# The loads of the first six tiles in the order of the program text

## The chip, the cores and the metric

The kernel runs on one core of a Trainium2 chip. A time is the device time in microseconds from the first to the last instruction of one execution. Where several runs are given, the median is taken.

## The reference

Four batches, eight heads, 768 positions, head size 64. Each head attends to 8 global positions and to the last 96 positions, with a linear penalty on the distance. The heads' results, joined to 512 features, go through a feed-forward block with a time shift.

```python
scores = scale * np.matmul(q, k.transpose(0, 1, 3, 2)) - slopes * dist
scores = np.where(keep, scores, -1000000000.0)
a = softmax(scores)
x = np.matmul(a, v)                      # heads joined: [4, 768, 512]
xk = mu_k * x + (1.0 - mu_k) * x_prev    # x_prev: x one position earlier
xr = mu_r * x + (1.0 - mu_r) * x_prev
k = np.maximum(xk @ w_k, 0.0)
out = sigmoid(xr @ w_r) * (k * k @ w_v)
```

`w_k` is 512 x 1024, `w_v` 1024 x 512, `w_r` 512 x 512. They arrive as 64-bit words, two 32-bit integers for each value.

## The kernel before

**Tiles.** The 4 x 768 positions are 24 tiles of 128. A tile is loaded (`load_tile`: q and k; `load_v`: v, as `va` and `vb`), then goes through `scores` in four pairs of heads (L424 to L428 on TensorE, bias and row maximum on VectorE at L433, exponential on ScalarE at L434, scaling by the reciprocal `r` on GpSimd at L450 or ScalarE at L448), `transposes` (L462, copied by ScalarE at L464) and `weighted`, the products with v (L481, copied to `x` at L492). Tiles 0 to 5 use q and k as they are loaded (64 partitions, names `qz` and `kz`); later ones are split in a high and a low part first (`qraw`, `kraw`, L297 on GpSimd, L403 and L404 on VectorE).

**Feed-forward.** Two tiles make a chunk. `mix` forms xk and xr with a high and a low part (L505 to L510); the low part of the first chunk's xk is `xk_lo`, on VectorE at L510. `channel_mix` multiplies with the weights in three products each (L517, L518, L519): `kp` for w_k, `z` for w_r, `vps` for w_v. The second product of each `kp` step (L518) reads `xk_lo`.

**Weights.** Ten blocks of 1 MB, w_0 to w_3 of `w_k`, w_4 and w_5 of `w_r`, w_6 to w_9 of `w_v`. `weight_load` brings one in (L181, L182). `weight_begin` makes a 32-bit float of the two integers in three steps on VectorE (L210, L211, L212) and casts it to the high part on ScalarE (L216). `weight_end` makes the low part: over TensorE (L230, L231), or by a subtraction at L234, on VectorE, and for w_4 and w_5 on GpSimd. The table `PLAN` says which.

**Order.** The program text is a loop over steps; each step loads the next tile, runs the score stage of one tile, the value products of an earlier one, some of the feed-forward, and one or two weight blocks. A scheduler takes the instructions in this order, estimates when each could start, and places them anew on each engine's queue. What an engine executes is then that fixed order. All loads go through SyncE's one queue, where an instruction that has to wait holds those behind it. A load waits for the readers of its buffer (q has two buffers, `qz_0` and `qz_1`, k three, v two), and for the landing of an earlier load whose semaphore it takes over; there are eight of these.

Of the kernel before, what the change touches and what calls it, by code (L numbers as in the profile page):

```python
# [62 lines left out]
def tile_biased_attention_channel_mix(ctx: ExitStack, tc: tile.TileContext, qT, kT, v, n_sizes, mu_kr, w_k, w_v, w_r, q_rows, k_rows, v_rows, slopes, out):  # L63
# [215 lines left out]
    def weights_load(n):  # L279
        while w_count[2] < min(n, len(w_steps)):  # L280
            weight_load(w_count[2])
            w_count[2] += 1

    def weights_go(begun, ended):
        weights_load(begun)
        while w_count[0] < min(begun, len(w_steps)):
            weight_begin(w_count[0])
            w_count[0] += 1
        while w_count[1] < min(ended, w_count[0]):
            weight_end(w_count[1])  # L290
            w_count[1] += 1
# [41 lines left out]
    def first_keys(n):  # L333
        if n % NT:
            (vec.tensor_copy if n in PLAN.get("KC", ()) else pool_copy)(state[n - 1]["kr"][0:64, :, 128 - OWN : 128 - BACK], k_first)
        else:
            pool_copy(k_first, state[n]["kr"][0:64, :, 0:GMAX])

    def load_tile(n):
        b, t = divmod(n, NT)  # L340
        s = state[n] = {}
        native = n < NATIVE
        halves = (0,) if native else (0, 64)
        if native:
            qr, kr = q_zero[n % 2], k_ring[n % 3]
        else:
            qr = p4k.tile([128, H, 128], F32, tag="t4k", name=f"qraw_{n}")
            if n == NATIVE:
                kr = kw_pool.tile([128, H, W], F32, tag="kw", name=f"kraw_{n}")
            else:  # L350
                kr = p4k.tile([128, H, 128], F32, tag="t4k", name=f"kraw_{n}")
        for o in halves:
            q_load[n] = nc.sync.dma_start(qr[o : o + 64], qT[n])
        for o in halves:
            if n == NATIVE:
                nc.sync.dma_start(kr[o : o + 64, :, OWN:W], kT[n])
                if t:
                    nc.sync.dma_start(kr[o : o + 64, :, 0:GMAX], kT[n - t, :, :, 0:GMAX])
                    nc.sync.dma_start(kr[o : o + 64, :, GMAX:OWN], kT[n - 1, :, :, 32:128])
            else:  # L360
                nc.sync.dma_start(kr[o : o + 64], kT[n])
        s["qr"], s["kr"] = qr, kr

    def load_v(n):

        g = PLAN.get("VB", {}).get(n)
        if g in q_load:
            with tc.issue_after(q_load[g].ins):
                load_v_now(n)
        else:  # L370
            load_v_now(n)
# [14 lines left out]
    def split_tile(n):  # L386
        t = n % NT
        s = state[n]
        s["sum"] = s_pool.tile([128, H], F32, name=f"sum_{n}", tag="sum")
        s["nmax"] = s_pool.tile([128, H], F32, name=f"nmax_{n}", tag="nmax")  # L390
        s["e"] = {}
        if n < NATIVE:
            return
        qh = q_pool.tile([128, H, 128], F32R, name=f"qh_{n}", tag="qh")
        ql = q_pool.tile([128, H, 128], F32R, name=f"ql_{n}", tag="ql")
        kw = kw_pool.tile([128, H, W], F32R, name=f"kw_{n}", tag="kw")
        cur = kw[:, :, 0 if n == NATIVE and t else OWN : W]
        kr = s["kr"]
        if n == NATIVE:
            kr = kr[:, :, W - cur.shape[2] : W]  # L400
        pool_copy(qh, s["qr"])
        pool_copy(cur, kr)
        vec.tensor_sub(ql, s["qr"], qh)  # L403
        vec.tensor_sub(cur[64:128], kr[64:128], cur[64:128])  # L404
        if t and n > NATIVE:
            pk = state[n - 1]["kw"]
            first = OWN if t == 1 else 0
            pool_copy(kw[:, :, GMAX:OWN], pk[:, :, OWN + 32 : W])
            pool_copy(kw[:, :, 0:GMAX], pk[:, :, first : first + GMAX])
        s["qh"], s["ql"], s["kw"] = qh, ql, kw  # L410
# [41 lines left out]
    def transposes(n, hp):  # L452
        s = state[n]
        parts = [128, W - 128] if n % NT else [128]
        nb = len(parts)
        pt = ps_t.tile([128, 512], F32, name=f"t_{n}_{hp}", tag="t")
        et = et_pool.tile([128, 512], F32, name=f"et_{n}_{hp}", tag="et")
        for u in range(2):
            e = s["e"].pop(2 * hp + u)
            for k, p in enumerate(parts):  # L460
                c = (2 * k + u) * 128
                pe.transpose(pt[0:p, c : c + 128], e[:, k * 128 : k * 128 + p], ident)  # L462
        for k, p in enumerate(parts):
            (vec.tensor_copy if (n, hp, k) in PLAN.get("ET", ()) else act.copy)(et[0:p, k * 256 : k * 256 + 256], pt[0:p, k * 256 : k * 256 + 256])  # L464
        s["et", hp] = et

    def weighted(n, hp):
        t = n % NT
        s = state[n]
        if hp == 0:  # L470
            s["av"] = ps_a.tile([128, 512], F32, name=f"av_{n}", tag="av")
        et = s.pop(("et", hp))
        blocks = s["va"]
        nb = len(blocks)
        for u in range(2):
            h = 2 * hp + u
            for k, vt in enumerate(blocks):

                q, c, p = k * LATE, (2 * k + u) * 128, vt.shape[0]
                o = s["av"][64 * u : 64 * u + 64, hp * 128 + q : (hp + 1) * 128]  # L480
                pe.matmul(o, vt[:, h * 64 : (h + 1) * 64], et[0:p, c + q : c + 128], start=k == 0, stop=k == nb - 1)  # L481
        if hp == 3:
            c, i = divmod(n, 2)
            if i == 0:
                xt = x_pool.tile([128, 4, 257], F32, name=f"x_{c}", tag="x")
                state["x", c] = xt
                if t == 0:
                    pool.memset(xt[:, :, 0:1], 0.0)
                else:
                    pool_copy(xt[:, :, 0:1], state["x", c - 1][:, :, 256:257])  # L490
            xt = state["x", c]
            (vec.tensor_copy if n in PLAN.get("XC", ()) else act.copy)(xt[:, :, 1 + 128 * i : 129 + 128 * i], s["av"].rearrange("p (a q) -> p a q", a=4))  # L492
# [81 lines left out]
    def ffn(c):  # L574
        xt = state["x", c]
        xk = mix(xt[:, :, 1:257], xt[:, :, 0:256], "k", p4k, f_pool, c < PLAN.get("MA", 1))
        xr = mix(xt[:, :, 1:257], xt[:, :, 0:256], "r", p4k, f_pool, c < PLAN.get("MA", 1))
        return channel_mix(xk, xr, lambda i: out[(2 * c + i) * 128 : (2 * c + i + 1) * 128, :], f_pool, f2_pool, ps_f, c >= 10, c == NCHUNK - 1)
# [7 lines left out]
    def run_ffn(amount):  # L586
        budget[0] += amount
        while budget[0] >= 1.0 and queue:
            try:
                next(queue[0])  # L590
                budget[0] -= 1.0
            except StopIteration:
                queue.pop(0)
        if not queue:
            budget[0] = 0.0

    load_tile(0)
    split_tile(0)
    for step in range(NTILES + 1):
        if step + 1 < NTILES:  # L600
            load_tile(step + 1)
        if step == 0:
            load_v(0)
        if step < NATIVE:
            first_keys(step)
        for hp in range(4):
            if hp == 0 and step > 1:
                for i in range(4):
                    weighted(step - 2, i)
            if hp == 0 and 0 < step < NTILES:  # L610
                load_v(step)
            if step:
                transposes(step - 1, hp)
            if step < NTILES:
                scores(step, hp)
            if hp == 0:
                if step >= LAG and (step - LAG) % 2 == 0:
                    queue.append(ffn((step - LAG) // 2))
                    if len(queue) == 1 and step == LAG:
                        budget[0] = PLAN.get("BUD", -17.5)  # L620
            run_ffn(2.5)
            run_ffn(2.5)
            if hp == 1 and step + 1 < NTILES:
                split_tile(step + 1)
            slot = 4 * step + hp
            weights_load(LOADS[min(slot, len(LOADS) - 1)])
            n = BEGUN[min(slot, len(BEGUN) - 1)]
            weights_go(n, n - 1 if slot < len(BEGUN) else n)
# [194 lines left out]
```

## Time and profile before

| | |
|---|---|
| median of 3 runs | 503.87 us (503.28 to 503.95) |
| the profiled execution, its span | 503.9 us |
| TensorE busy | 488.8 us, 97% |
| VectorE busy | 355.8 us, 71% |
| ScalarE busy | 344.6 us, 68% |
| GpSimd busy | 234.2 us, 46% |
| DMA moved | 60.57 MB, mean 120 GB/s |
| granted clock of TensorE | 0.998 |

The shares are means over the whole span. The first 50 us differ from the rest: there the weights and six tiles are loaded and the weights are prepared. In the rows, PE is TensorE, DVE VectorE, ACT ScalarE, POOL GpSimd and SP SyncE; an arrow [idle before <- releaser] gives the idle time just before an instruction and what ended it.

### The profile page before, as it was taken

What the parts mean: (1) busy time and instruction counts of PE and PEld (TensorE: products, weight loads), DVE (VectorE), ACT (ScalarE), POOL (GpSimd) and SP (SyncE); (2) the same over time, 40 slices, a digit from 0 to 9 for tenths busy, and PEclk for the clock granted to TensorE, in tenths of its full rate; (3) what the DMA queues carried; (4) which work ended last, traced back from release to release, by engine and by line L of the source; (5) the groups of instructions that cost most, each with busy time, mean ns of one, the idle gap of its engine ahead of it and who ended that gap; (6) DMA issues with size and microseconds to landing.
All of it is one profiled execution on the core that took longest, in us unless ns stands there. A gap on an engine that the chain in (4) does not pass through costs nothing.

```text
span 503.9 us, 10303 instructions
## 1 busy us (share of the span) xinstructions
PE 488.8 (97%) x3590; PEld 431.3 (86%) x3590; DVE 355.8 (71%) x843; ACT 344.6 (68%) x858; POOL 234.2 (46%) x371
## 2 busy tenths in 40 slices
PE   7978999999999999999999999999999999999996
PEld 4647988998998998998898998898898898897985
DVE  5999989868678668658678668658768755457441
ACT  7798888377587577567577677667577678587360
POOL 4537537645655635626546536527447435204000
PEclk9999999999999999999999999999999999999999
DMA  8999460714604604603603612613413215647311
GB/s 224 325 252 250 133 182 18 195 54 104 165 1 115 167 5 103 171 14 82 159 29 86 165 39 81 160 46 81 132 59 79 86 39 164 208 159 260 125 43 48
DMA packets 22586, 60.57 MB, mean 120 GB/s; under 512 B 3296, under 2 KB 4576, under 8 KB 22016
## 3 DMA queue, kind: packets, MB, share of 16 engines
q1 hardware_dynamic: 22384, 59.85, 41.5%
q8 instruction: 30, 0.49, 0.4%
q14 instruction: 28, 0.23, 0.2%
q10 hardware_dynamic: 144, 0.00, 0.0%
HBM read 53.55 MB, written 6.29 MB: 119 GB/s over the span
## 4 chain that ended last, share of the span: by engine, by line
PE 84%; DMA 7%; DVE 4%; POOL 3%; issue 1%; SPq 0%; POOLq 0%; DVEq 0%
PE kp L517 8%; PE vps L518 8%; PE vps L519 8%; PE kp L519 8%; PE vps L517 8%; PE kp L518 8%; PE av L481 7%; PE t L462 7%; PE z L517 4%; PE z L519 4%; PE z L518 4%; DMA qz<-in_qT_dram 4%; PE s L428 3%; PE s L427 3%; DMA qraw<-in_qT_dram 2%; POOL e L450 2%
## 5 line engine op out<-in xcount | busy, mean ns | idle before, releaser
L450 POOL TENSOR_SCALAR e<-e,r 128x232 f32<-128x232 f32 (+1 forms) x180 | 94.9, 545 | 152.5 <-DVE r L444 121.5
L517 PE MATMUL kp<-xk_hi,wk 128*128 128x256 f32 x384 | 108.4, 283 | 0.0
L518 PE MATMUL kp<-xk_lo,wk 128*128 128x256 f32 x384 | 107.3, 280 | 0.5 <-DVE xk_lo L510 0.5
L519 PE MATMUL kp<-xk_hi,wk 128*128 128x256 f32 x384 | 107.4, 280 | 0.0
L434 ACT ACTIVATE e<-e,nmax 128x232 f32<-128x232 f32 (+1 forms) x192 | 90.0, 472 | 24.6 <-DVE nmax L433 22.4
L433 DVE CUSTOM_DVE_ANT_0 e<-s,pat 128x232 f32<-128x232 f32 (+1 forms) x192 | 64.7, 374 | 18.6 <-PE s L428 15.7
L517 PE MATMUL vps<-wv,kk_hi 128*128 128x512 f32 (+1 forms) x200 | 76.7, 384 | 0.0
L519 PE MATMUL vps<-wv,kk_lo 128*128 128x512 f32 (+1 forms) x200 | 76.6, 383 | 0.0
L518 PE MATMUL vps<-wv,kk_hi 128*128 128x512 f32 (+1 forms) x200 | 76.4, 382 | 0.1
L518 PEld LDWEIGHTS kp<-xk_lo,wk 128*128 128x128 f32 x384 | 72.1, 188 | 1.3 <-DVE xk_lo L510 0.7
L517 PEld LDWEIGHTS kp<-xk_hi,wk 128*128 128x128 f32 x384 | 72.1, 188 | 0.8 <-issue 0.2
L519 PEld LDWEIGHTS kp<-xk_hi,wk 128*128 128x128 f32 x384 | 72.1, 188 | 0.0
L464 ACT COPY et<-t 128x256 f32<-128x256 f32 (+1 forms) x176 | 57.0, 373 | 8.1 <-PE t L462 7.5
L545 DVE TENSOR_TENSOR kk<-kp,kk 128x512 f32<-128x512 f32 x48 | 33.1, 689 | 40.8 <-ACT kk L544 40.5
L462 PE MATMUL t<-ident,e 128*128 128x128 f32 x352 | 55.9, 277 | 1.7 <-POOL e L450 1.6
L462 PEld LDWEIGHTS t<-ident,e 128*128 128x128 f32 x352 | 40.2, 135 | 12.3 <-POOL e L450 2.6
L547 DVE TENSOR_TENSOR kk_lo<-kk,kk_hi 128x512 fp32r<-128x512 f32 x48 | 34.0, 709 | 23.3 <-ACT kk_hi L546 23.0
L403 DVE TENSOR_TENSOR ql<-qraw,qh 128x1024 fp32r<-128x1024 f32 x18 | 35.1, 1951 | 13.7 <-POOL qh L297 13.7
L519 PEld LDWEIGHTS vps<-wv,kk_lo 128*128 128x128 f32 x200 | 37.6, 188 | 7.5
L518 PEld LDWEIGHTS vps<-wv,kk_hi 128*128 128x128 f32 x200 | 37.7, 189 | 6.6 <-DVE wv L234 0.2
L517 PEld LDWEIGHTS vps<-wv,kk_hi 128*128 128x128 f32 x200 | 37.7, 189 | 6.5 <-issue 0.2
L492 ACT COPY x<-av 128x512 f32<-128x512 f32 x24 | 14.2, 591 | 42.5 <-PE av L481 42.5
(115 smaller groups left out, 1105.6 us busy)
## 6 DMA issues: line engine op xcount, KB each, us to landing
qraw<-in_qT_dram SPq DMA_DIRECT2D x36, 256.0 KB
kraw<-in_kT_dram SPq DMA_DIRECT2D x36, 256.0 KB
out_dram<-sig SPq DMA_DIRECT2D x23, 256.0 KB
va<-in_v_dram SPq DMA_DIRECT2D x20, 240.0 KB
vb<-in_v_dram SPq DMA_DIRECT2D x20, 208.0 KB
w<-in_w_k_dram SPq DMA_DIRECT2D x4, 1024.0 KB
w<-in_w_v_dram SPq DMA_DIRECT2D x4, 1024.0 KB
again<-in_w_k_dram SPq DMA_DIRECT2D x8, 512.0 KB
```

Of the source, the lines that this page charges most:

```text
L403: vec.tensor_sub(ql, s["qr"], qh)
L433: biased[n, hp] = vec.tensor_tensor_reduce(out=e[:, :w], in0=o, in1=p[:, h, :], op0=ALU.add, op1=ALU.min, scale=-0.125, scalar=3.0e38, acc ...
L434: act.activation(e[:, :w], e[:, :w], AF.Exp, bias=s["nmax"][:, h : h + 1], scale=-1.0, accum_out=s["sum"][:, h : h + 1])
L450: pool.tensor_scalar(e[:, :w], e[:, :w], r[:, u : u + 1], 1.0, op0=ALU.mult, op1=ALU.mult)
L462: pe.transpose(pt[0:p, c : c + 128], e[:, k * 128 : k * 128 + p], ident)
L464: (vec.tensor_copy if (n, hp, k) in PLAN.get("ET", ()) else act.copy)(et[0:p, k * 256 : k * 256 + 256], pt[0:p, k * 256 : k * 256 + 256])
L481: pe.matmul(o, vt[:, h * 64 : (h + 1) * 64], et[0:p, c + q : c + 128], start=k == 0, stop=k == nb - 1)
L517: pe.matmul(o, sh, mh, start=first, stop=False)
L518: pe.matmul(o, sh, ml, start=False, stop=False)
L519: pe.matmul(o, sl, mh, start=False, stop=last)
L545: vec.tensor_mul(kk, pv, kk)
L547: rest = vec.tensor_sub(kkl[:, 2 * fp : 2 * fp + 2, :], kk, kkh[:, 2 * fp : 2 * fp + 2, :])
```

## The change

A mode of the scheduler that leaves an engine's instructions in the order of the program text is switched on for SyncE, before the first tile is loaded, and off again at step 6.

```diff
+    queue_order = ExitStack()
+    queue_order.enter_context(tc.manual_schedule(engines={mybir.EngineType.SP}))
     load_tile(0)
     split_tile(0)
     for step in range(NTILES + 1):
+        if step == 6:
+            queue_order.close()
         if step + 1 < NTILES:
             load_tile(step + 1)
```

On SyncE, from the blocks w_2 and w_3 (`w64_2`, `w64_3`) on; `qz_1` and `kz_0` are q and k of tile 3, `qz_0` and `kz_1` those of tile 4. Before:

```order
L181 DMA w64_2_300<-in_w_k_dram 128x2048
L181 DMA w64_3_357<-in_w_k_dram 128x2048
L383 DMA vb_2_405<-in_v_dram 104x512
L182 DMA w64_4_456<-in_w_r_dram 128x2x1024
L182 DMA w64_5_517<-in_w_r_dram 128x2x1024
L361 DMA kz_0_179<-in_kT_dram 64x1024
L353 DMA qz_1_182<-in_qT_dram 64x1024
L381 DMA va_2_404<-in_v_dram 8x512
L382 DMA va_2_404<-in_v_dram 120x512
L361 DMA kz_1_183<-in_kT_dram 64x1024
L353 DMA qz_0_178<-in_qT_dram 64x1024
```

The same stretch of the change:

```order
L181 DMA w64_2_302<-in_w_k_dram 128x2048
L181 DMA w64_3_359<-in_w_k_dram 128x2048
L353 DMA qz_1_182<-in_qT_dram 64x1024
L361 DMA kz_0_179<-in_kT_dram 64x1024
L381 DMA va_2_406<-in_v_dram 8x512
L382 DMA va_2_406<-in_v_dram 120x512
L383 DMA vb_2_407<-in_v_dram 104x512
L182 DMA w64_4_458<-in_w_r_dram 128x2x1024
L182 DMA w64_5_519<-in_w_r_dram 128x2x1024
L353 DMA qz_0_178<-in_qT_dram 64x1024
L361 DMA kz_1_183<-in_kT_dram 64x1024
L381 DMA va_3_549<-in_v_dram 8x512
```

q and k of tile 3, and `va_2`, moved from behind w_4 and w_5 to a place ahead of them. Further up in the queue, q of tile 2 now stands ahead of k of tile 2 and `va_1`.

On VectorE, the twelve rows that end with the first chunk's `xk_lo` (`wa_5` is block w_5 in preparation, `e_3_1` head 1 of tile 3). Before:

```order
L508 SCALAR_TENSOR_TENSOR mix_k_571<-x_0_401,mus_69,mix_k_571 128x256
L211 SCALAR_TENSOR_TENSOR wa_5_519<-w64_5_517,wa_5_519 128x1024
L433 ISA e_3_0_565,nmax_3_455<-s_3_0_560,pat_136 128x232
L433 ISA nmax_3_455 128x1
L433 ISA e_3_1_568,nmax_3_455<-s_3_0_560,pat_136 128x232
L433 ISA nmax_3_455 128x1
L212 SCALAR_TENSOR_TENSOR wa_5_519<-w64_5_517,wa_5_519 128x1024
L433 ISA e_3_2_610,nmax_3_455<-s_3_1_605,pat_136 128x232
L433 ISA nmax_3_455 128x1
L433 ISA e_3_3_613,nmax_3_455<-s_3_1_605,pat_136 128x232
L433 ISA nmax_3_455 128x1
L510 TENSOR_TENSOR xk_lo_573<-mix_k_571,xk_hi_572 128x1024
```

With the change, eleven rows from the first step of w_5 on:

```order
L210 TENSOR_SCALAR wa_5_521<-w64_5_519 128x1024
L433 ISA e_3_3_615,nmax_3_457<-s_3_1_607,pat_136 128x232
L433 ISA nmax_3_457 128x1
L212 SCALAR_TENSOR_TENSOR wa_4_460<-w64_4_458,wa_4_460 128x1024
L508 SCALAR_TENSOR_TENSOR mix_k_573<-x_0_403,mus_69,mix_k_573 128x256 x2
L433 ISA e_3_4_642,nmax_3_457<-s_3_2_637,pat_136 128x232
L433 ISA nmax_3_457 128x1
L433 ISA e_3_5_645,nmax_3_457<-s_3_2_637,pat_136 128x232
L433 ISA nmax_3_457 128x1
L211 SCALAR_TENSOR_TENSOR wa_5_521<-w64_5_519,wa_5_521 128x1024
L508 SCALAR_TENSOR_TENSOR mix_k_573<-x_0_403,mus_69,mix_k_573 128x256 x2
```

and, three rows further down, the twelve that end with `xk_lo`:

```order
L433 ISA nmax_3_457 128x1
L443 TENSOR_SCALAR r_3_1_618<-sum_3_456 128x4
L212 SCALAR_TENSOR_TENSOR wa_5_521<-w64_5_519,wa_5_521 128x1024
L210 TENSOR_SCALAR wa_6_648<-w64_6_627 128x1024
L433 ISA e_4_0_739,nmax_4_626<-s_4_0_734,pat_136 128x232
L433 ISA nmax_4_626 128x1
L433 ISA e_4_1_742,nmax_4_626<-s_4_0_734,pat_136 128x232
L433 ISA nmax_4_626 128x1
L444 RECIPROCAL r_3_1_618<-r_3_1_618 128x4
L210 TENSOR_SCALAR wa_7_781<-w64_7_696 128x1024
L211 SCALAR_TENSOR_TENSOR wa_6_648<-w64_6_627,wa_6_648 128x1024
L510 TENSOR_TENSOR xk_lo_575<-mix_k_573,xk_hi_574 128x1024
```

All of tile 3's bias steps, those of tile 4's first two heads, the first two steps of w_6 and the first of w_7 now stand ahead of `xk_lo`. On TensorE, the first three pairs of tile 4's scores, the last transposes of tile 2 and eleven of tile 2's sixteen value products moved ahead of the first L518. From tile 6 on the order is the same but for the buffer numbers.

## Rows read from the trace of the kernel before

**Rows 1.** Busy time by stretch, core 0: us, then busy (xinstructions) of each engine

```profile
20.00:46.20 26.20, 21.88 (x155) 16.32 (x153) 25.02 (x55) 23.13 (x64) 15.39 (x16) 1.00 1.00 290
46.20:95.00 48.80, 47.12 (x355) 41.35 (x356) 44.37 (x92) 38.07 (x93) 26.75 (x31) 1.00 0.48 130
95.00:400.00 305.00, 305.00 (x2292) 274.15 (x2290) 221.52 (x515) 208.82 (x517) 162.38 (x260) 1.00 0.34 93
400.00:503.90 103.90, 99.25 (x716) 88.81 (x712) 51.11 (x120) 60.12 (x139) 20.42 (x39) 0.99 0.39 130
sum 503.90, PE 488.82 PEld 431.28 DVE 355.76 ACT 344.56 POOL 234.25; mean PE 97.76 PEld 86.26 DVE 71.15 ACT 68.91 POOL 46.85
```

**Rows 2.** Waits of TensorE over the span: in total, times, longest

```profile
PE s L424 <- DMA qz<-in_qT_dram: 2.5, 1, 2.5
...
PE t L462 <- POOL e L450: 1.6, 2, 0.8
...
PE s L424 <- issue: 0.7, 1, 0.7
```

**Rows 3.** Timeline of SyncE's queue, 16 to 40 us: start, us, what

```profile
19.49 0.54 SPq L353 DMA_DIRECT2D qz<-in_qT_dram  x1
...
38.47 0.90 SPq L182 DMA_DIRECT2D w<-in_w_v_dram  x2
```

**Rows 4.** The chain that ended last, in order of time: start, us, piece

```profile
19.49 18.96 DMA qz<-in_qT_dram
...
39.72 0.20 PE s L424 x2
39.92 0.24 PE s L425 x2
...
41.07 0.45 PE t L462 x4
...
49.82 0.31 DVE e L433
...
51.59 0.61 DVE wa L210
...
52.27 0.39 DVE mix_r L508
52.66 1.14 DVE wa L212
...
93.82 1.80 PE av L481 x32
```

**Rows 5.** Timeline of VectorE to 95 us: start, us, instruction [idle before, releaser]

```profile
35.60 0.71 DVE L210 TENSOR_SCALAR wa<-w 128x1024 int32<-128x1024 int32 x1 [0.27 <-DMA w<-in_w_r_dram]
...
39.34 1.21 DVE L211 SCALAR_TENSOR_TENSOR wa<-w,wa 128x1024 int32<-128x1024 int32 x1
...
42.95 3.22 DVE L510 TENSOR_TENSOR xk_lo<-mix_k,xk_hi 128x1024 fp32r<-128x1024 f32 x1
46.10 3.08 DVE L210 TENSOR_SCALAR wa<-w 128x1024 int32<-128x1024 int32 x1
...
59.83 1.19 DVE L510 TENSOR_TENSOR xr_lo<-mix_r,xr_hi 128x1024 fp32r<-128x1024 f32 x1
```

**Rows 6.** Timeline of GpSimd to 95 us

```profile
39.21 3.50 POOL L450 TENSOR_SCALAR e<-e,r 128x232 f32<-128x232 f32 x3 [2.06 <-DVE r L444]
42.68 2.40 POOL L234 TENSOR_TENSOR wr<-wa,wr 128x1024 fp32r<-128x1024 f32 x1
...
46.23 2.40 POOL L234 TENSOR_TENSOR wr<-wa,wr 128x1024 fp32r<-128x1024 f32 x1
```

**Rows 7.** Busy time by stretch: the last two columns are DMA share and GB/s

```profile
30.00:36.00 6.00, 4.66 (x35) 2.57 (x30) 5.73 (x13) 5.97 (x19) 2.22 (x3) 1.00 1.01 198
...
48.00:50.00 2.00, 1.29 (x11) 0.85 (x11) 2.00 (x6) 0.90 (x4) 0.63 (x1) 1.00 0.61 127
```

**Rows 8.** Timeline of TensorE, 46 to 92 us

```profile
46.22 0.39 PE L518 MATMUL kp<-xk_lo,wk 128*128 128x256 f32 x1 [0.49 <-DVE xk_lo L510]
```

## The prediction

> **What bounds the kernel now.** I read busy time by stretch first, then the waits of TensorE, the chain of waits, and last the timelines of SyncE, VectorE and GpSimd from 16 to 64 us. The span is 503.9 us and TensorE is busy for 488.8 of it [rows 1]. By stretch its idle time lies at the two ends. From 95 to 400 us there is none (305.00 of 305.00), so whatever is late there is late behind TensorE [rows 1]. The last stretch holds 4.65 idle us (103.90 less 99.25), which belongs to the end of the kernel. The change can touch 20 to 46.2 us (26.20 less 21.88, 4.32 idle) and 46.2 to 95 us (48.80 less 47.12, 1.68 idle) [rows 1]. Six microseconds, 1.2% of the span, is therefore all that a better order of loads can win. A loss has no such bound.
>
> The longest wait in there is the one that the moved loads bear on: tile 3's scores wait 2.5 us for its q [rows 2]. The chain has that transfer as one piece of 18.96 us from 19.49, when SyncE issued it behind the two w_r blocks (w_4 and w_5) of 1 MB each [rows 3, 4]. The reader should see a second thing there. When q has landed, the chain doesn't stay on TensorE: it goes through the subtraction xk_lo on VectorE (42.95 to 46.2), and the first feed-forward products (kp) start 0.05 us behind it, at 46.22, after a wait for just that [rows 5, 8]. From there on TensorE has work enough. What ends the starved stretch is thus the time of the first xk_lo; an earlier q matters as far as it brings that forward.
>
> **The change part by part.** It adds and removes no work; it fixes the SyncE order of tiles 0 to 5, and the scheduler then places the other engines' instructions anew.
>
> SyncE. q and k of tile 3 move ahead of w_4 and w_5, as the order shows; so does va of tile 2. k of tile 2 and va of tile 1 move back behind q of tile 2, which waits for tile 0's scores. I cost that last move at nothing: w_0 and w_1 (2.1 MB) are still under way then and cover it. The same transfers as before stand ahead of w_2 and w_3. q of tile 3 is then no longer behind w_4 and w_5, and its 2.5 us of waiting go. For w_4 and w_5 it is a new wait on SyncE: they now leave behind that q, which has to wait for tile 1's scores (19.49 before). w_6 and w_7 left at 38.47, behind q's landing [rows 3]; now they stand behind va of tile 3, which waits for tile 1's value products. Both waits I cost at nothing, as the DMA engines were busy at a share of 1.00 from 20 to 46.2 us [rows 1], so that a transfer issued earlier only queues longer; the cover is gone if the queue runs dry, and then each microsecond of it counts in full.
>
> What is late next is w_5. Before, VectorE took it at 35.60 after 0.27 of waiting, and q of tile 3 had landed at 38.45 [rows 4, 5]. By then w_4, w_5, k and q were all in. Now w_5 is the last of that set. Lower bound for its landing: 35.5, if the moved transfers cost it nothing. Upper bound: 38.45 plus va of tile 2, 0.25 MB, 1.2 us at the 198 GB/s of 30 to 36 us [rows 7], so 39.7. The nearest row is the landing at 38.45, and I take 38.5.
>
> VectorE. In the new order xk_lo stands behind more work. From the first step of w_5's preparation (L210) up to and with xk_lo there are now 3 L210, 4 of L211 and L212, 7 bias steps (L433), 4 mix steps (L508), 2 small ones and xk_lo. By the pieces of the chain 0.61, 1.14, 0.32 (0.31 and its accumulator read) and 0.39 us [rows 4], 0.1 at most for a small one, and xk_lo without its hold as its sister xr_lo, 1.19 [rows 5]: 1.8 + 4.6 + 2.2 + 1.6 + 0.2 + 1.2 = 11.6 us. Before, the same stretch had one L210, three of L211 and L212 and four bias steps.
>
> One cost comes on top. xk_lo took 3.22 us before, where xr_lo took 1.19, since it began 0.3 us after GpSimd's subtraction wr (42.68, 2.40 us); the L210 at 46.10 took 3.08 beside the second wr [rows 5, 6]. In the new order the first wr needs ScalarE's cast of w_4, which needs w_4's L212; that ends 2.1 us (0.61 + 0.32 + 1.14) behind w_5's landing. L211 of w_5 starts 3.5 us behind it, and so the two meet. What that does to L211 the trace does not show. Bounds: nothing, as the L211 at 39.34 kept its 1.21 us beside GpSimd's scaling of e [rows 5, 6]; or 2.0, as xk_lo. The instruction on GpSimd is the same subtraction, so I take 2.0.
> The Trainium skill, SBUF — State Buffer, section "Who interferes with whom", says that a VectorE instruction with two SBUF inputs and a GpSimd instruction that reads SBUF exclude each other for a whole instruction, and whichever comes second blocks; by that rule L211 would pay the 2.0; the row at 39.34 does not bear it out, and by that row alone the sum would be 2.0 us lower, 502.8.
>
> So xk_lo ends at 38.5 + 11.6 + 2.0 = 52.1, and kp starts at 52.1 where it started at 46.2.
>
> TensorE. It is not idle all that time: the new order puts work ahead of kp that used to follow it. These are tile 4's first three pairs of scores, 3 x 2 x (0.20 + 0.24) = 2.6 us; the last four transposes of tile 2, 0.45; and 11 of the 16 value products of tile 2, 11/16 of 1.80 = 1.2, all by pieces of the chain [rows 4]. Together 4.3 us. A kp start at 46.2 + 4.3 = 50.5 would leave as much idle time ahead of it as before. At 52.1 there are 1.6 us more.
>
> Behind kp, two waits are seen before: 0.7 (no releaser shown, right behind the held L210) and 0.8, the longer of the two waits of transposes for GpSimd [rows 2]. The first goes, since tile 4's scores come earlier. The second I keep: the scaling of e on GpSimd still stands between VectorE's steps. w_8, w_9 and tile 6's q also leave earlier, but TensorE hardly waited there, so I count nothing for them; the cover is its own queue of kp, z and vps products, and if VectorE fell behind that, the price would be up to the 0.8 again.
>
> Sum: 1.6 - 0.7 = +0.9 us on the profiled 503.9, which is the median of the runs (503.87) to the last digit shown: 504.8 us.
>
> **The rivals.**
> Faster. w_5 lands near its old time and L211 is not held. Then xk_lo would end at 35.5 + 11.6 = 47.1, but L210 of w_7 now stands ahead of it, so w_7 must be in. The DMA engines are busy until about 49.2 (0.61 of the stretch 48 to 50) [rows 7]; behind w_7 come only k and q of tile 5, 0.52 MB, 2.6 us at 198 GB/s. w_7 is in at 46.6 at the earliest; L210, L211 and xk_lo after it make 49.5. That is 1.0 below break-even, and both waits behind kp may go, 1.5: 501.4 at best, 502.3 with half a microsecond on each. For it: VectorE waited little for weights before. Against it: w_4 to w_7 all have the moved transfers ahead of them, and VectorE has no slack.
>
> Slower. The second wr holds xk_lo. It follows three scalings of e, which wait for the reciprocal that in the new order stands just ahead of w_7's L210. The three took 3.50 us at 39.21 [rows 6]; xk_lo ends 2.9 behind that reciprocal. So the hold comes if w_7 lands more than some 0.6 us behind the reciprocal. Price 2.0: 506.8, and 508.0 with w_5 at 39.7. By the sum above the reciprocal ends at 49.2, so w_7's landing decides, after or before 49.8 or so. For it: this pair met before. Against: the DMA engines were through at 49.2 with more to move.
>
> The order does nothing of note: tile 3's scores start earlier, and xk_lo, held by w_5 to w_7, comes at 50.5 to 51.5, the idle time only changing place. 503.9, half a microsecond to either side.
>
> **How the numbers follow.** Two measurements of this kernel can be told apart from about 0.2%, 1.0 us. Forecast (504.8, own range 503.7 to 505.9): 0.40, of which 0.17 falls within 0.2% and 0.23 above. Faster rival: 0.24, nearly all below 502.9. Slower rival: 0.20. Nothing of note: 0.16, all within. So faster 0.24, same 0.33, slower 0.43. The range runs from 501.9, which keeps most of the faster case, to 507.8, just under the slower one's end.
>
> **What would show it.** Right: tile 3's first scores near 31 to 34 us with no wait for q; VectorE's waits for w_r blocks longer than 0.27; w_5's L210 at 37 to 40; a held L211 behind it; the first L518 of kp at 51 to 53 with the three pairs of tile 4's scores ahead of it; no idle time on TensorE from 100 us. Wrong: kp at or before 49.5, which makes it faster; or kp near 51 and more than 2 us of waits between 55 and 95, which makes it slower by another way than the one here.

## The result, and the profile after

The change makes the kernel slower. Beside the kernel before on one chip: 510.74 us against 503.91 (medians of 4 runs each), ratio 1.0100 with a 95% interval of 1.0061 to 1.0140. (The medians alone would give 1.0136; the measured ratio is lower, and one of the four runs before took 508.75 us.) On a second chip: 509.68 (8 runs) against 505.16 (31 runs), ratio 1.0077, 1.0050 to 1.0103. The forecast was 504.8 with a range up to 507.8; both medians lie above it. The sign was the likelier one of the forecast, the size is several times too small.

One remark on the base. In all runs that list both, the time is the span plus 1.7 to 1.9 us. By this the profiled execution of before, with its span of 503.9, was some 1.8 us slower than the median run; that is an estimate, as its own time is not listed. Profile against profile the change costs 4.1 us (508.0 less 503.9), 0.8%, about what the second chip's ratio says. These are two single executions, though: on the second chip the spans of the kernel before alone ran from 501.6 to 506.4 us.

TensorE is as busy as before: 488.9 us against 488.8. By this count all of the 4.1 us is idle time; work at half speed counts as busy in it, which the last section comes back to. By stretch (columns as in [rows 1]; the second and third lines divide at the start of kp):

```profile
20.00:46.20 26.20, 22.11 (x156) 17.89 (x155) 20.62 (x48) 21.36 (x62) 12.24 (x15) 0.87 1.03 278
46.20:56.58 10.38, 4.37 (x43) 3.73 (x41) 9.03 (x18) 5.29 (x15) 4.06 (x4) 0.98 0.82 239
56.58:95.00 38.42, 38.42 (x267) 34.52 (x268) 36.24 (x73) 32.07 (x71) 16.38 (x25) 0.96 0.36 95
95.00:400.00 305.00, 305.00 (x2293) 274.03 (x2292) 221.52 (x511) 207.36 (x512) 159.18 (x257) 1.00 0.35 93
400.00:508.00 108.00, 103.32 (x747) 92.43 (x745) 53.67 (x124) 62.47 (x149) 24.65 (x44) 0.99 0.38 127
```

From 20 to 46.2 us TensorE idles 4.09 us; it was 4.32 [rows 1]. Then come 6.01 idle us up to 56.58, where before kp had been running since 46.22 [rows 8]. Behind kp there is none up to 95; before there were 1.68 [rows 1]. The tail is as it was (4.68, 4.65). So 6.01 less 1.68 and 0.23 makes the 4.1; at the start and in the tail the difference is 0.1 or less.

The waits of TensorE in total (times, longest) name what took the place of q's 2.5 us [rows 2]:

```profile
PE kp L518 <- DVE xk_lo L510: 5.3, 1, 5.3
PE s L424 <- DVE nmax L433: 5.3, 4, 3.1
...
PE t L462 <- POOL e L450: 1.0, 1, 1.0
```

The wait for q is gone, and a wait of 3.1 us for VectorE stands in its stead. VectorE's timeline shows why (compare [rows 5]):

```profile
33.86 0.69 DVE L210 TENSOR_SCALAR wa<-w 128x1024 int32<-128x1024 int32 x1 [0.17 <-DMA w<-in_w_r_dram]
...
36.11 0.09 DVE L433 DVE_READ_ACCUMULATOR2_ANT nmax<- 128x1 f32 x1
39.19 0.69 DVE L210 TENSOR_SCALAR wa<-w 128x1024 int32<-128x1024 int32 x1 [2.99 <-DMA w<-in_w_r_dram]
39.80 0.39 DVE L433 CUSTOM_DVE_ANT_0 e<-s,pat 128x232 f32<-128x232 f32 x1
...
42.68 3.42 DVE L211 SCALAR_TENSOR_TENSOR wa<-w,wa 128x1024 int32<-128x1024 int32 x1
...
49.90 0.17 DVE L444 RECIPROCAL r<-r 128x4 f32<-128x4 f32 x1
51.42 0.69 DVE L210 TENSOR_SCALAR wa<-w 128x1024 int32<-128x1024 int32 x1 [1.35 <-DMA w<-in_w_v_dram]
52.03 3.35 DVE L211 SCALAR_TENSOR_TENSOR wa<-w,wa 128x1024 int32<-128x1024 int32 x1
55.31 1.21 DVE L510 TENSOR_TENSOR xk_lo<-mix_k,xk_hi 128x1024 fp32r<-128x1024 f32 x1
```

VectorE waits 2.99 us for w_5, and behind that L210 in its queue stands a bias step (39.80) that TensorE's next scores wait for. The wait for q has become a wait for w_5, at about the same time (the scores behind it start at 40.25, before at 38.59) and a little longer. Then L211 of w_5 takes 3.42 us, L210 of w_7 waits 1.35 us for its block, L211 of w_6 takes 3.35 us, and only then comes xk_lo. The two long L211 stand beside GpSimd's subtractions, as [rows 6] shows them for before:

```profile
42.63 2.39 POOL L234 TENSOR_TENSOR wr<-wa,wr 128x1024 fp32r<-128x1024 f32 x1
50.24 1.32 POOL L450 TENSOR_SCALAR e<-e,r 128x232 f32<-128x232 f32 x3 [5.22 <-DVE r L444]
51.53 2.77 POOL L234 TENSOR_TENSOR wr<-wa,wr 128x1024 fp32r<-128x1024 f32 x1
```

The Trainium skill, SBUF — State Buffer, section "Who interferes with whom", says that a VectorE instruction with two SBUF inputs contends with a GpSimd instruction that reads SBUF, and that the order of issue decides who blocks. The trace agrees: both L211 start after a wr and last 3.42 and 3.35 us, where the same step lasts 1.23 alone.

The chain that ended last runs through the same steps, where in [rows 4] it ran through q (start, us, piece):

```profile
34.59 16.73 DMA w<-in_w_v_dram
51.42 0.69 DVE wa L210
52.11 3.28 DVE wa L211
55.39 1.15 DVE xk_lo L510
56.58 0.58 PE kp L518
```

### The profile page after: what moved, and what is told of

It is laid out like the page before. It is cut to its first block, busy times and chain, and to the rows that moved or that the text cites. A ratio compares the mean times of both kernels' runs of the same rounds, so it can differ in the third digit from the quotient of the medians.

```text
span 508.0 us, 10303 instructions
## 1 busy us (share of the span) xinstructions
PE 488.9 (96%) x3590; PEld 432.8 (85%) x3590; DVE 356.7 (70%) x843; ACT 344.5 (68%) x858; POOL 226.3 (45%) x371
## 4 chain that ended last, share of the span: by engine, by line
PE 88%; DMA 8%; DVE 2%; SPq 1%; issue 0%; DVEq 0%
PE kp L517 9%; PE kp L518 9%; PE kp L519 9%; PE vps L517 9%; PE vps L519 9%; PE vps L518 9%; PE av L481 7%; PE t L462 7%; PE z L517 5%; DMA w<-in_w_k_dram 4%; PE z L519 4%; PE z L518 4%; DMA w<-in_w_v_dram 3%; PE s L428 3%; PE s L427 3%; DVE wa L211 1%
## 5 line engine op out<-in xcount | busy, mean ns | idle before, releaser
L450 POOL TENSOR_SCALAR e<-e,r 128x232 f32<-128x232 f32 (+1 forms) x180 | 88.9, 512 | 165.0 <-DVE r L444 122.0
L518 PE MATMUL kp<-xk_lo,wk 128*128 128x256 f32 x384 | 108.0, 281 | 5.3 <-DVE xk_lo L510 5.3
L518 PEld LDWEIGHTS kp<-xk_lo,wk 128*128 128x128 f32 x384 | 72.8, 189 | 6.0 <-DVE xk_lo L510 5.5
L518 PE MATMUL vps<-wv,kk_hi 128*128 128x512 f32 (+1 forms) x200 | 76.3, 382 | 0.0
L518 PEld LDWEIGHTS vps<-wv,kk_hi 128*128 128x128 f32 x200 | 37.7, 189 | 6.3
```

The costliest lines, as they stand in the source:

```text
L450: pool.tensor_scalar(e[:, :w], e[:, :w], r[:, u : u + 1], 1.0, op0=ALU.mult, op1=ALU.mult)
L518: pe.matmul(o, sh, ml, start=False, stop=False)
```

## The experiments

All were timed against the kernel before on their own chip. The times to compare are the ratios, since the kernel before itself had medians of 504.32, 505.16 and 505.37 us on the three occasions.

**xk_lo ahead of w_6 and w_7.** The change, with a table entry that puts the first steps of these two blocks behind xk_lo.

```diff
-    "BEHIND": {},
+    "BEHIND": {6: 0, 7: 0},
```

> The changed kernel with one edit: the preparation of w_6 and w_7 on VectorE is told to stand behind the first xk_lo. The order of the loads stays as in the change. Theory (the placing of xk_lo behind w_7 and the held step L211 of w_6 makes the loss): xk_lo can start when the L212 of w_5, two bias steps and a small one are done, at about 49.4 us by the trace of the change, so kp starts at 50.6 instead of 56.6, TensorE's 5.3 us wait for xk_lo falls under 1 us, the clock stays at 2.4 GHz from there, and the time falls by 5 to 7 us, to 504 to 506. Rival (the loads themselves come too late, so whatever stands behind them is late): kp starts little earlier, and the time stays within 2 us of the change, at 508.5 or more.

506.64 us, ratio 1.0043 (1.0029 to 1.0058). xk_lo ends at 50.5 instead of 56.5, and TensorE comes to the first kp product with xk_lo at 50.91 without waiting for it. About half of the loss is gone (1.0043 against 1.0077 and 1.0100), so the place of w_6 and w_7 ahead of xk_lo made about half of it. TensorE's waits that are left are for bias steps, those behind w_5's L210 and its held L211 above all:

```profile
PE s L424 <- DVE nmax L433: 6.5, 3, 3.1
```

The time came out 0.6 us above the expected 506.

**No subtraction on GpSimd.** The change, with the low parts of w_4 and w_5 made on VectorE.

```diff
-    "LOW": 'PPDPGGDDDD',
+    "LOW": 'PPDPDDDDDD',
```

> The changed kernel with one edit: the two subtractions that make the low parts of w_4 and w_5 go from GpSimd to VectorE (1.14 us each). Theory (GpSimd's subtraction holds VectorE's steps with two inputs, 2.2 us twice ahead of xk_lo): no L211 longer than 1.3 us; xk_lo ends near 51.2, since one subtraction of 1.14 us now stands ahead of it, kp at 51.3 instead of 56.6; time 504 to 506. Rival (the long L211 come from elsewhere, or xk_lo waits for w_7 anyway): kp not before 54, time 508 or more.

507.13 us, ratio 1.0046 (1.0031 to 1.0062). In VectorE's timeline no L211 is held, and kp follows xk_lo on TensorE:

```profile
42.33 1.22 DVE L211 SCALAR_TENSOR_TENSOR wa<-w,wa 128x1024 int32<-128x1024 int32 x1
...
51.12 1.22 DVE L510 TENSOR_TENSOR xk_lo<-mix_k,xk_hi 128x1024 fp32r<-128x1024 f32 x1
```

```profile
52.39 0.58 PE L518 MATMUL kp<-xk_lo,wk 128*128 128x256 f32 x1 [2.25 <-DVE xk_lo L510]
```

The same step that took 3.42 us takes 1.22 with GpSimd's subtraction gone, so the hold is shown and not only argued. The time is not the price of the hold alone: the scheduler also placed w_7's L210 behind xk_lo here (52.51). It is 1.1 us above the upper end of what was expected, and kp came at 52.39 instead of 51.3.

**q of tile 3 ahead of w_4, in the kernel before.** The edit orders these two; all else stays with the scheduler.

```diff
-    "WB": {},
+    "WB": {4: 3},
```

> The kernel before with one part of the change: the load of w_4 is placed behind that of tile 3's q, nothing else is fixed on SyncE. The scheduler then places xk_lo behind the first step of w_7, as in the change. Theory (this move alone brings the loss, through the placing of VectorE's steps): kp starts at 52 to 56, time 507 to 510. Rival (the loss needs the rest of the fixed order, as the early wait for tile 2's q or w_6 behind va of tile 3): 503 to 505.

508.86 us, ratio 1.0071 (1.0048 to 1.0094). This one edit costs most of what the whole change costs. It is not q alone that moved, though: on SyncE k of tile 3 and `va_2` now leave ahead of w_4 too, so the stretch has the later part of the change's order.

```profile
17.07 0.47 SPq L361 DMA_DIRECT2D kz<-in_kT_dram  x1
17.64 0.54 SPq L353 DMA_DIRECT2D qz<-in_qT_dram  x1
18.28 0.44 SPq L381 DMA_DIRECT2D va<-in_v_dram  x1
...
19.15 3.67 SPq L182 DMA_DIRECT2D w<-in_w_r_dram  x2
```

w_5 comes in at 38.54, VectorE waits for w_7, that L210 is held beside GpSimd's wr, and kp starts at 57.22. The wait of TensorE ahead of it is not for xk_lo but for a bias step behind that L210:

```profile
38.54 0.69 DVE L210 TENSOR_SCALAR wa<-w 128x1024 int32<-128x1024 int32 x1 [2.34 <-DMA w<-in_w_r_dram]
...
50.52 2.51 DVE L210 TENSOR_SCALAR wa<-w 128x1024 int32<-128x1024 int32 x1 [1.89 <-DMA w<-in_w_v_dram]
...
54.73 1.21 DVE L510 TENSOR_TENSOR xk_lo<-mix_k,xk_hi 128x1024 fp32r<-128x1024 f32 x1
```

```profile
50.08 2.40 POOL L234 TENSOR_TENSOR wr<-wa,wr 128x1024 fp32r<-128x1024 f32 x1
```

```profile
53.81 0.72 PE L424 MATMUL s<-kz,qz 128*128 128x104 f32 x2 [5.42 <-DVE nmax L433]
```

The expected kp was 52 to 56; the time was inside its range.

**Only the early loads in program order.** The change, with the mode switched off at step 2: the queue is that of the change up to w_3 and that of before from there.

```diff
-        if step == 6:
+        if step == 2:
```

> The changed kernel with the fixed order ended at step 2 instead of 6: only tile 2's q is moved ahead of its k and of tile 1's v; w_4 and w_5 leave ahead of tile 3's q as before. Here xk_lo stands behind two steps of w_6, not behind w_7. Theory: tile 3's q lands at 38 to 39 us again, kp starts at 48 to 52, time 503.5 to 506. Rival (the early wait for tile 2's q makes the loss): 509 or more.

506.17 us, ratio 1.0029 (1.0013 to 1.0045), kp at 50.49, inside its range; the time is 0.2 us above its own, and q of tile 3 landed at 36.7 us instead of 38 to 39. I had costed the early moves at nothing; in this run they cost 0.3% by themselves. The scheduler answers them, too, with a block's steps ahead of xk_lo, and one of these is held:

```profile
46.23 3.00 DVE L211 SCALAR_TENSOR_TENSOR wa<-w,wa 128x1024 int32<-128x1024 int32 x1
49.25 1.19 DVE L510 TENSOR_TENSOR xk_lo<-mix_k,xk_hi 128x1024 fp32r<-128x1024 f32 x1
```

```profile
45.76 2.40 POOL L234 TENSOR_TENSOR wr<-wa,wr 128x1024 fp32r<-128x1024 f32 x1 [1.78 <-ACT wr L216]
```

**The change again.** No edit.

> The change itself, timed beside the kernel before on the chip of the other runs. Theory (the kernel loses what its first kp loses): kp near 56.6 us as in its first profile, held L211 of w_5 and w_6 (over 3 us each), a span near 508 and 1.0% over before. Rival (the first runs of it were unlucky, its order itself costs what the prediction said): 0.2% over before, kp near 52.

509.68 us, ratio 1.0077 (1.0050 to 1.0103), kp at 56.40: the first measurement repeats. Its second hold fell one step earlier, on L210 of w_7 (51.15, 2.92 us) and not on L211 of w_6 (1.21 us); the two together cost the same within 0.1 us. Which VectorE step meets the subtraction is a matter of tenths of a microsecond; in both traces one meets it. Whether one always does is open: two of the eight runs took 507.0 and 507.3 us, the other six 509.5 to 510.6, and no trace says what the two did differently.

**Both undone.** The change with both edits, BEHIND for w_6 and w_7 and no subtraction on GpSimd.

> The change with the first steps of w_6 and w_7 behind xk_lo and all low parts of w_r made on VectorE instead of GpSimd, so neither the landing of w_7 nor a hold by the subtraction stands ahead of kp. The two edits alone took some 4.1 and 3.6 us off the change. Theory (both act on the one start of kp, and TensorE has other waits there): kp near 49.6 us, 505.0 to 506.5 us, hardly better than one alone. Rival (they are separate costs, which add up): 502.7 to 503.5 us, under before.

506.42 us, ratio 1.0026 (1.0007 to 1.0046), kp at 49.31. On the start of kp the two edits don't add up: each alone took 5.7 and 4.2 us off its 56.6, both together 7.3. They act on one start, as the theory had it. In time the runs can't tell: added to each other, the gains of the two alone (1.0043 and 1.0046) would make 1.0012 from the second chip's 1.0077, which lies inside this interval.

**Only w_7 behind xk_lo.** L211 of w_6 stays ahead of xk_lo, GpSimd keeps its subtraction.

```diff
-    "BEHIND": {},
+    "BEHIND": {7: 0},
```

> The change with the first step of w_7 alone put behind xk_lo; the L211 of w_6 stays ahead of it and GpSimd keeps the subtraction. Theory (the wait for w_7 is what pushes the L211 of w_6 under the second wr): the L211 begins near 50.0, ahead of wr, and takes 1.2 us, xk_lo follows and ends near 52.4, kp near 52.4, 506.5 to 507.5 us. Rival (the hold comes whatever w_7 does, since GpSimd follows VectorE's reciprocal): L211 or xk_lo takes over 3 us, kp at 54.4 or later, 508 us or more.

507.08 us, ratio 1.0039 (1.0024 to 1.0053). On VectorE, GpSimd and TensorE:

```profile
50.02 1.19 DVE L211 SCALAR_TENSOR_TENSOR wa<-w,wa 128x1024 int32<-128x1024 int32 x1
51.13 1.21 DVE L510 TENSOR_TENSOR xk_lo<-mix_k,xk_hi 128x1024 fp32r<-128x1024 f32 x1
```

```profile
50.26 5.64 POOL L450 TENSOR_SCALAR e<-e,r 128x232 f32<-128x232 f32 x3 [5.22 <-DVE r L444]
55.87 2.58 POOL L234 TENSOR_TENSOR wr<-wa,wr 128x1024 fp32r<-128x1024 f32 x1
```

```profile
52.39 0.39 PE L518 MATMUL kp<-xk_lo,wk 128*128 128x256 f32 x1 [1.11 <-DVE xk_lo L510]
```

This is the cleanest of them, and as expected in each number. The one instruction that waits for w_7 moved from ahead of xk_lo to behind it, and L211 of w_6 begins before GpSimd's next work and keeps its 1.19 us; now it is GpSimd that is slowed (5.64 us for three scalings that took 1.32). The second wr slips to 55.87, behind xk_lo. On the same chip the change cost 0.77% and this 0.39%.

**No subtraction on GpSimd, in the kernel before.** The same `LOW` entry as above.

> The kernel before with all low parts of w_r made on VectorE instead of GpSimd. Theory (the first xk_lo sets the end of the starved stretch there too, and the subtraction holds it for 2.0 us): xk_lo takes 1.2 us, kp starts 1 to 2 us earlier than 46.2, 502.5 to 503.5 us. Rival (the queue of loads and TensorE's other waits set it, an earlier kp only moves the idle time): within 0.2% of before, or slower by the 1.1 us that VectorE takes over.

504.57 us, ratio 0.9988 (0.9971 to 1.0004). xk_lo takes 1.21 us from 44.21, but kp starts at 46.83, when TensorE has come through what is ahead of it. The rival was right: there the hold was nearly hidden. The edit isn't free of cost, as one subtraction now stands on VectorE ahead of xk_lo, which ended only some 0.8 us earlier.

**w_4 and w_5 back ahead of q of tile 3.** The change, program order kept, with the two blocks issued earlier in the text.

```diff
-    "LOADS": (2, 2, 2, 2, 3, 3, 4, 4, 4, 5, 5, 6, 6, 7, ...
+    "LOADS": (2, 2, 2, 2, 3, 3, 4, 6, 6, 6, 6, 6, 6, 7, ...
```

> The change with w_4 and w_5 moved back ahead of q and k of tile 3, in program order otherwise: the first tiles' loads keep the new order, the later ones the old. Theory (the change is two costs that add up: q of tile 3 ahead of w_4, measured alone at 0.7%, and the order of the first three tiles, measured alone at 0.3%): w_5's L210 at 35 to 36.5 us, kp near 50, 0.2 to 0.4% over the kernel before, 505 to 506.5 us. Rival (the order of the first tiles costs nothing by itself, and the three loads ahead of w_4 are all of it): kp at 46 to 47.5, within 0.2% of before.

506.36 us, ratio 1.0016 (0.9999 to 1.0033), kp at 49.86. The kp start is that of the theory. The ratio lies just under its 0.2 to 0.4% and can't be told from no change, and w_5's L210 came sooner than expected, at 33.74: with w_5 early, it is again the steps of w_6 that stand ahead of xk_lo, its L210 at 44.85 after 1.50 us of waiting. With the later part (q, k and `va_2` ahead of w_4) at 1.0071 and the early part at 1.0029 or 1.0016, the two make about the change's 1.0077 to 1.0100; but the later part alone is not told apart from it, so that the two add up is not shown.

**Low parts of w_4 and w_5 over TensorE, in the kernel before.**

```diff
-    "LOW": 'PPDPGGDDDD',
+    "LOW": 'PPDPPPDDDD',
```

> The kernel before with the low parts of w_4 and w_5 made over TensorE instead of by GpSimd's subtraction, so neither xk_lo nor the L210 behind it is held and VectorE gets no new work. Theory (an earlier end of xk_lo pays only as far as TensorE has nothing else to wait for): xk_lo takes 1.2 us and kp starts 1 to 2 us earlier, but TensorE has some 2 us of products more, so within 0.2% of before. Rival (the hold on VectorE is worth its full 4 us): 501 to 502.5 us, faster than both kernels.

508.59 us, ratio 1.0056 (1.0032 to 1.0081). Both expectations missed. xk_lo is in early (42.91, 1.22 us), but TensorE has more to do ahead of kp, and its first product with xk_lo is at 52.96. TensorE is busy from 40 to 70 us without a gap; its total is 494.25 us against 488.82 [rows 1]. Work given to TensorE to spare VectorE comes back in the time: 5.4 us more of it, and a span 2.8 us longer (506.7 against 503.9).

Put in order of kp's start, the runs are nearly in order of time: 46.8 us, 0.9988; 49.3, 1.0026; 49.9, 1.0016; 50.5, 1.0029; 50.9, 1.0043; 52.4, 1.0039 and 1.0046; 56.4 and 56.6, 1.0077 and 1.0100; 57.2, 1.0071. (The last kernel, with other work on TensorE, is left out.) No version beats the kernel before by more than its interval.

## Why the prediction was wrong

*kp's start decides.* It held up. Nine kernels with kp between 46.8 and 57.2 us follow it to some 0.3%, and there is no idle time from 95 to 400 us in the change. That xk_lo is what ends the starved stretch held in the change, but not everywhere: in three of the kernels (kp at 46.83, 50.91 and 57.22) TensorE came to kp without waiting for it.

*The wait for q goes.* Right, and worth nothing: I took the 2.5 us as gone ahead of kp and did not look at who stands behind w_5's L210 on VectorE. The bias step there passed the wait on to TensorE, 3.1 us.

*w_5 lands at 38.5.* 39.19, inside the bounds, 0.7 late.

*11.6 us of VectorE steps, and 2.0 for a first hold.* From w_5's L210 to the end of xk_lo are 17.3 us: 11.6 of steps, 2.2 of the first hold, 1.35 of waiting for w_7, 2.1 of a second hold. The steps and the first hold were sized rightly. The trace of before had a row that spoke against that hold, and it was no guide: the L211 that kept its 1.21 us [rows 5] stood beside a scaling, not beside a subtraction. The rule of the Trainium skill cited there gave the right sign.

*Nothing later holds it.* This is the step that failed. I took w_7 to be in at 46.6 to 49.2; it landed at 51.42. The slower rival had the mechanism and the point from which it decides (w_7 after 49.8), at a chance of 0.20 and a price of 2.0. The hold fell on the instruction ahead of xk_lo and not on xk_lo, which changes nothing. The point rested on three scalings of 3.50 us; here they took 1.32 (50.24), and wr stood 1.5 us behind the reciprocal. And the price left out the wait for w_7 itself. It should have been 1.35 + 2.1. With 0.7 of w_5, 0.2 of the first hold and these, 52.1 becomes 56.5; kp was at 56.58. The run with w_7 alone moved takes this step by itself: kp at 52.39, where I had put it (w_5 was 0.8 us later there, and that L210's 0.6 us no longer stood ahead), and 2.0 us over before (0.39% of 505.16).

*Break-even at 50.5.* Near enough for the change: 56.58 less 50.5 is 6.1, and the idle time ahead of kp grew by 5.7. There is luck in this: from 20 us to kp TensorE's busy time grew by 4.6 us (22.11 and 4.37 less 21.88), near the 4.3 of moved work, although part of the work ahead of kp now ran at half speed (last section); elsewhere TensorE must have been quicker by as much, and no run says where. With the kp that I had forecast the loss was still more than 0.9. There the time behind kp failed: I counted 0.7 as saved, but in the run with kp at 52.39 the idle time from kp to 400 us was 1.60 (42.61 less 41.76, 305.00 less 304.25), as much as before.

```profile
52.39:95.00 42.61, 41.76 (x304) 36.57 (x305) 40.85 (x77) 30.22 (x72) 29.84 (x31) 1.00 0.47 128
95.00:400.00 305.00, 304.25 (x2271) 272.97 (x2270) 221.30 (x513) 208.87 (x517) 160.52 (x259) 1.00 0.34 92
```

In the change those waits did go, all 1.68 of them. How late kp is doesn't settle it alone: without the subtraction on GpSimd kp stood at 52.39 too, and TensorE had no idle time from there to 400 us.

*The early moves cost nothing.* Wrong by 0.3% in the run with only these (1.0013 to 1.0045), by a held step ahead of xk_lo that TensorE waited 2.77 us behind. In the other kernel that has them, with w_4 back, the cost is not told apart from none.

One sum was off by 0.1: the faster rival's 502.3 is 502.4 by its own terms. Nothing hangs on it.

*Why w_7 was late* stays partly open. It left 4 us earlier than before (34.15 against 38.47 [rows 3]) and needed 16.73 us. From 46 to 51.4 us the DMA engines were busy at a mean share of 0.71, so they were not all at work while it was still out:

```profile
46.00:51.40 5.40, 4.57 (x44) 3.93 (x42) 4.07 (x15) 5.12 (x14) 1.16 (x3) 1.00 0.71 171
```

A landing worked out from busy shares and bytes over a mean rate, as I did, was then too early. Which engines held its last packets the profile does not show, and no run asked it.

## What to carry to other kernels

Before crediting a wait that goes, look at what the freed transfer pushes back, and at every instruction queued behind the new waiter: an in-order engine hands its wait on to whoever needs the next instruction. A wait and a hold that meets because of it are one price, not two alternatives. And where a scheduler replans the engines, a change to one queue is also a change to the order on the others; here that order, with the hold that it brought, took most of the time: with the loads as in the change and both undone, 0.26% of its 0.77% was left.

## What else the runs showed of the hardware

TensorE's granted clock fell behind its idle stretches. In the change it idled from 37.1 to 40.25 us and then worked at half speed, 1.2 GHz, to 46; it idled from 51.25 to 56.58, and the first dozen kp products came 0.21 us apart instead of 0.12, some 1.1 us more in all.

```profile
40.00:46.00 6.00, 5.75 (x34) 5.26 (x35) 6.00 (x10) 3.33 (x9) 2.60 (x2) 0.51 1.04 295
...
56.00:58.00 2.00, 1.42 (x6) 1.43 (x7) 2.00 (x4) 1.44 (x4) 0.00 (x0) 0.52 1.01 408
```

A wait of one length did both: the 2.5 us for q left the clock at 1.00 in the kernel before, and at 0.50 from 38 to 40 us in the last experiment (the same wait, 2.48 us). What the first slow stretch of the change cost, the kernel with xk_lo ahead of w_6 and w_7 shows. TensorE has the same instructions there, waited 2.95 us at 40.29 for the same bias step, and its clock stayed at 1.00. It was through sooner and then waited 3.11 us for the next bias step, where the change waited 0.69 us:

```profile
40.00:44.00 4.00, 3.71 (x39) 3.46 (x40) 4.00 (x10) 3.12 (x10) 1.79 (x2) 1.00 1.03 267
44.00:47.40 3.40, 0.36 (x4) 0.17 (x2) 3.40 (x8) 1.23 (x4) 0.91 (x1) 1.00 1.01 257
...
47.48 0.47 PE L424 MATMUL s<-kz,qz 128*128 128x104 f32 x2 [3.11 <-DVE nmax L433]
```

The change, at the same scores:

```profile
47.59 0.47 PE L424 MATMUL s<-kz,qz 128*128 128x104 f32 x2 [0.69 <-DVE nmax L433]
```

These scores start at 47.48 and at 47.59, so by these two traces the slow stretch took the place of a wait and cost 0.1 us. It also hides idle time in the sum of the section on the result: the kernel that kept its clock has 486.7 us of TensorE in all, the change 488.9. The mean clock doesn't order the kernels either: without the subtraction on GpSimd it is 0.989, as in the change, and the span is 506.1 against 508.0. What the second slow stretch cost, behind kp, no run takes apart.

A held VectorE step need not have two inputs. L210, with one, took 2.92 us beside wr when the change was run again, and 2.51 in the run with q of tile 3 ahead of w_4, as it took 3.08 in [rows 5]. The section of the Trainium skill named above counts tensor_scalar among the operations that can enter modes in which they contend with GpSimd; these three rows agree that it does. What the Trainium skill says of the order of issue, as cited in the section on the result, two of them do not bear out, as far as the trace's starts go: L210 began ahead of wr (51.15 against 51.18 us, and 46.10 against 46.23 in [rows 5, 6]) and was the one that was held.
